# Which queue issues the weights' loads during the attention stage

## The chip, the cores and the metric

One core of one Trainium2 chip runs the whole kernel. The metric is the device time in microseconds (us) of one execution. The kernel before was timed in three runs: median 664.88 us, from 664.65 to 665.11.

## The reference

Sparse-window attention feeds two feed-forward layers, all in float32:

```python
# attention: 2 batches, 8 heads, 768 tokens, 64 columns per head
k_sum = k.reshape(B, H, 24, 32, D).max(axis=3)      # one key per block of 32
v_sum = v.reshape(B, H, 24, 32, D).mean(axis=3)     # one value per block
scores = concat(where(|i - j| < 16, q @ k.T / 8, -1e9), q @ k_sum.T / 8 + log(32))
x = softmax(scores) @ concat(v, v_sum)               # 1536 tokens x 512
# first layer, 512 -> 2048 -> 512
h = x @ w_in;  x = (h * sigmoid(1.702 * h)) @ w_out
# second layer, 512 -> 1536 -> 512
x = (sigmoid(x @ w_gate) * (x @ w_val)) @ w_out2
```

The weights arrive in a 64-bit format and every product of the layers is formed from a high and a low part of both factors.

## The kernel before, in words

**Attention** works in 24 units: two batches, three groups of 256 query rows, four pairs of heads (`units`). A unit needs its query tile (`load_q`, 256 KB, five buffers), its pair's keys (`load_k`, 400 KB for one batch and pair), a window of values (`load_v`, 768 KB for a group of units) and the block means of the values, copied into the same window (`put_v`, 256 KB, from the tile `vs`, which is computed from the loads `vt`). The steps of a unit are listed in `ORDER` with a lag each: `w_copy` (L370, GpSimd) scales the keys, `b_pe` (L379, L381, TensorE) makes the scores `ps_s`, `b_max` (L386, VectorE) the row maximum `nm`, `b_exp` (L394, ScalarE) the exponentials, `n_inv` (L401, L403, VectorE) and `n_mul` (L408, GpSimd) divide by the sum, `c_pe` (L414, TensorE) transposes, `c_copy` (L419, VectorE) copies to `pt`, `d_pe` (L429, TensorE) multiplies with the values, and `d_hi`, `d_lo` (L447, L450) split the result into `xH` and `xL`. `c_pe` and `d_pe` come three units after `b_pe`.

**Weights.** A matrix here is one piece of 256 columns or rows of a layer's weight. `fetch` (L145 to L156) issues two loads for it, `raw` (1024 KB) and `mid` (the same memory shifted by one 16-bit word, 1023 KB). `decode` (L92 to L120) makes the high and low parts from both in six VectorE steps (L104, L108, L110, L112, L117, L119) and two of ScalarE. There is one buffer `raw` and one buffer `mid`; the second matrix alone lies in `xH` and `xL`, which are still free then. `load_group` (L158) decodes the matrices in turn, and behind the second step of each decode it calls `fetch` for the matrix two places on. So the load of a matrix into `raw` must wait until VectorE has read the last one there (L104), and the load into `mid` until L108 has read it.

**The attention stage** (the first `manual_schedule` block) calls `fetch` twice ahead of its loop, for the first and the second matrix. In its loop over t from -1, `pull(2)` advances the decode, and four more fetches come out of it: the third matrix at t = 1, the fourth at t = 5, the fifth at t = 8, the sixth at t = 12. From t = 10 on `filler` puts four steps of the first layer between the units (`EARLY = 4`). The rest of both layers follows in the second block.

**Order.** SyncE's queue (SP) runs in the order of the program text: all loads of the attention but the first four query tiles, which ScalarE issues, and all fetches go through it one after another; one that waits for a buffer holds what is behind it. The other engines' instructions, GpSimd's (POOL) among them, are put in an order by a planner that simulates the program. Each engine then runs its list in that order.

Of the kernel before, what the change touches and what calls it, by code (L numbers as in the profile page):

```python
# [29 lines left out]
def attention_moe_moe2_kernel(ctx: ExitStack, tc: tile.TileContext, ins: dict, out: bass.AP):  # L30
    nc = tc.nc
# [47 lines left out]
    def pool(slots, n, name):  # L79
        p = ctx.enter_context(tc.tile_pool(name=name, bufs=n, reuse_waits="tile"))  # L80
        for s in slots:
            s.add(p, n)
        return p
# [8 lines left out]
    def decode(raw, mid, hi_out, lo_out):  # L92

        n = raw.shape[1] // 2
        head = raw.rearrange("p (n t) -> p n t", t=2)[:, :, 1]
        tail = mid.rearrange("p (n t) -> p n t", t=2)[:, :, 0]
        a, b, c = (wtmp.tile([P, n], U32, tag=f"d{x}", name=f"d{x}") for x in "abc")  # L100
        af, cf = a.bitcast(F32), c.bitcast(F32)
        ts = nc.vector.tensor_scalar

        ts(out=af, in0=head.bitcast(F32), scalar1=F64_MAX, scalar2=-F64_MAX, op0=ALU.min, op1=ALU.max)  # L104
        nc.scalar.activation(af, af, AF.Copy, scale=REBIAS)
        yield

        ts(out=b, in0=tail, scalar1=0x01FFFFFF, scalar2=None, op0=ALU.bitwise_and)  # L108
        yield
        ts(out=c, in0=a, scalar1=3, scalar2=0x7FFFF000, op0=ALU.logical_shift_left, op1=ALU.bitwise_and)  # L110
        yield
        nc.vector.scalar_tensor_tensor(  # L112
            out=c, in0=a, scalar=0x80000000, in1=c, op0=ALU.bitwise_and, op1=ALU.bitwise_or
        )
        nc.scalar.copy(hi_out, cf)
        yield
        ts(out=a, in0=c, scalar1=0xFF800000, scalar2=None, op0=ALU.bitwise_and)  # L117
        yield
        nc.vector.scalar_tensor_tensor(out=lo_out, in0=b, scalar=2.0 ** -36, in1=af, op0=ALU.mult, op1=ALU.mult)  # L119
        yield  # L120
# [8 lines left out]
    def rows_of(w, g):  # L129
        n = GF * P  # L130
        return w[g * n:(g + 1) * n, :].rearrange("(f p) e -> p f e", p=P)

    def cols_of(w, g, words):
        n = GF * P * words
        return w[:, g * n:(g + 1) * n].rearrange("(c p) e -> p c e", p=P)
# [3 lines left out]
    for layer, g in groups:  # L139
        for i, w in enumerate(mats[layer]):  # L140
            last = i == len(mats[layer]) - 1
            src = [rows_of(x, g) if last else cols_of(x, g, n) for x, n in ((w.bitcast(U32), 2), (w.bitcast(U16), 4))]
            pieces.append((f"{layer}_{g}_{i}", *src))

    def fetch():  # L145

        if pieces:
            name, src, shifted = pieces.pop(0)
            n, m = src.shape[1], src.shape[2]

            homes = ((xp, "xH"), (xp, "xL")) if name == "1_0_1" else ((wraw, "raw"), (wraw, "mid"))
            raw, mid = (p.tile([P, n * m], U32, tag=t, name=f"{t}{name}") for p, t in homes)
            nc.sync.dma_start(out=raw.rearrange("p (a n) -> p a n", a=n), in_=src)
            to = mid.bitcast(U16).rearrange("p (a n) -> p a n", a=n)
            nc.sync.dma_start(out=to[:, :, 0:2 * m - 1], in_=shifted[:, :, 1:])
            raws.append((raw, mid, (P, n, m // 2)))  # L156

    def load_group(layer, g):  # L158
        tiles = weights[layer, g] = []
        ready[layer, g] = 0  # L160
        for i in range(len(mats[layer])):
            raw, mid, shape = raws.pop(0)
            hi, lo = (w_slots.tile(list(shape), F32R, f"w{layer}_{g}_{i}{x}") for x in "HL")
            tiles += [hi, lo]
            parts = decode(raw, mid, hi.rearrange("p a n -> p (a n)"), lo.rearrange("p a n -> p (a n)"))
            for step, _ in enumerate(parts):
                if step == 1:

                    fetch()
                yield  # L170
            ready[layer, g] += 1
            yield
# [17 lines left out]
    def first(layer, g, blk, batch=False):  # L190
        w = weights[layer, g]
        gh = gh_slots.tile([P, GF, TB], F32R, f"gh{layer}_{g}_{blk}")
        gl = gl_slots.tile([P, GF, TB], F32R, f"gl{layer}_{g}_{blk}")
        gt[layer, g, blk] = gh, gl

        def sigmoid(layer, ps):
            sg = sg_slots.tile([P, TB], F32, "sg")
            nc.scalar.activation(sg, ps, AF.Sigmoid, scale=1.702 if layer == 1 else 1.0)  # L198
            return sg

        def gated(f, ps, sg):
            nc.vector.tensor_tensor(out=sg, in0=ps, in1=sg, op=ALU.mult)  # L202
            nc.scalar.copy(gh[:, f, :], sg)  # L203
            nc.gpsimd.tensor_tensor(out=gl[:, f, :], in0=sg, in1=gh[:, f, :], op=ALU.subtract)  # L204

        if batch:
            held = []
            for f in range(GF):
                held.append(project(w[0], w[1], f, blk, "ps_h"))
                yield  # L210
            held = [(ps, sigmoid(layer, ps)) for ps in held]
            yield
            for f, (ps, sg) in enumerate(held):
                gated(f, ps, sg)
            yield
            return
        for f in range(GF):
            ps = project(w[0], w[1], f, blk, "ps_h")
            sg = sigmoid(layer, ps)
            if layer == 2:  # L220
                ps = project(w[2], w[3], f, blk, "ps_v")
            gated(f, ps, sg)
            yield
# [50 lines left out]
    def pull(n):  # L274
        for _ in range(n):
            if next(coming, True):
                break

    def need(layer, g, n):
        while ready.get((layer, g), 0) < n:  # L280
            pull(1)

    with tc.manual_schedule(engines={mybir.EngineType.SP}), ExitStack() as es:
# [180 lines left out]
        for _ in range(4):  # L464
# [14 lines left out]
        sum_load(0, 3)  # L479
        load_q(4, nc.sync)  # L480
        fetch()
        fetch()
        make_identity(nc, ident)

        nc.vector.memset(mask, 0.0)
# [8 lines left out]
            out=win, in_=win, pattern=[[0, NSLOT], [1, P - W0]], compare_op=ALU.is_gt, fill=NEG,  # L494
# [3 lines left out]
            out=win, in_=win, pattern=[[0, NSLOT], [-1, P - W0]], compare_op=ALU.is_gt, fill=NEG,  # L498
# [62 lines left out]
    with tc.manual_schedule(engines={mybir.EngineType.SP}):  # L561
        pool([w_slots], 4, "w_b")
        pool([gh_slots, gl_slots], 1, "g_b")
        pool([sg_slots], 2, "sg_b")
        acc_b = ctx.enter_context(tc.tile_pool(name="acc_b", bufs=1, reuse_waits="tile"))
        ps_o = ctx.enter_context(tc.tile_pool(name="ps_o", bufs=6, space=PSUM, reuse_waits="tile"))
        o_tag = "o"
        pull(1000)
        coming = load_group(*groups[2])
        pull(1)  # L570
        prev = None
        for step in steps[EARLY:]:
            layer, g, blk = step
            need(layer, g, len(mats[layer]) - 1)
            for _ in first(*step):
                pull(1)
            if prev:
                need(*prev[:2], len(mats[prev[0]]))
                for _ in second(*prev, prev[1] == ends[prev[0]]):
                    pull(1 if groups.index((layer, g)) + 1 < n1 else 2)  # L580
            prev = step
            nxt = groups.index((layer, g)) + 1
            if nxt < len(groups) and groups[nxt] not in ready and blk == (NTB - 1 if layer == 1 and g < 2 else 0):
                pull(1000)
                coming = load_group(*groups[nxt])
        for _ in second(*prev, True):
            pass
# [40 lines left out]
```

## Time and profile before

| | |
|---|---|
| median of 3 runs | 664.88 us |
| the profiled execution's own time | 663.71 us |
| its span | 661.9 us |
| TensorE (PE) busy | 631.7 us, 95% |
| VectorE (DVE) busy | 415.2 us, 63% |
| ScalarE (ACT) busy | 243.1 us, 37% |
| GpSimd (POOL) busy | 187.2 us, 28% |
| moved by DMA | 93.97 MB, mean 142 GB/s |

The span runs from the first to the last instruction of the trace; the execution's own time is 1.8 us longer. An engine's busy share is a mean over stages with different limits, so the stages are looked at one by one. "PEclk" is the clock that TensorE was granted, as a share of full speed; a matmul at half the clock counts as busy for longer. In a row of the stages "DMA share" is how busy the 16 DMA engines were.

### The profile page before, as it was taken

What the parts mean: (1) busy time and instruction counts of PE and PEld (TensorE: products, weight loads), DVE (VectorE), ACT (ScalarE), POOL (GpSimd) and SP (SyncE); (2) the same over time, 40 slices, a digit from 0 to 9 for tenths busy, and PEclk for the clock granted to TensorE, in tenths of its full rate; (3) what the DMA queues carried; (4) which work ended last, traced back from release to release, by engine and by line L of the source; (5) the groups of instructions that cost most, each with busy time, mean ns of one, the idle gap of its engine ahead of it and who ended that gap; (6) DMA issues with size and microseconds to landing.
All of it is one profiled execution on the core that took longest, in us unless ns stands there. A gap on an engine that the chain in (4) does not pass through costs nothing.

```text
span 661.9 us, 8251 instructions
## 1 busy us (share of the span) xinstructions
PE 631.7 (95%) x3168; PEld 515.1 (78%) x3170; DVE 415.2 (63%) x604; ACT 243.1 (37%) x498; POOL 187.2 (28%) x164
## 2 busy tenths in 40 slices
PE   6478799999999999999999999999999999999997
PEld 3255688778888888888888888888888888888886
DVE  6899656559998777777778626437627627422223
ACT  3355574746443333333345425313213213211110
POOL 6574576413332222213131112111111111211110
PEclk9778899999999999999999999999999999999999
DMA  9999773007775242434333034423414413000013
GB/s 314 351 372 325 223 236 94 3 13 276 255 261 198 93 171 99 159 111 145 118 138 111 20 124 143 147 92 140 176 66 151 182 49 128 0 1 0 13 67 112
DMA packets 39672, 93.97 MB, mean 142 GB/s; under 512 B 2128, under 2 KB 12624, under 8 KB 39632
## 3 DMA queue, kind: packets, MB, share of 16 engines
q1 hardware_dynamic: 39056, 92.39, 40.3%
q10 hardware_dynamic: 576, 1.05, 0.4%
q8 instruction: 25, 0.41, 0.2%
q14 instruction: 15, 0.12, 0.1%
HBM read 88.71 MB, written 3.15 MB: 139 GB/s over the span
## 4 chain that ended last, share of the span: by engine, by line
PE 88%; DVE 3%; DMA 3%; ACT 3%; POOL 1%; issue 1%; SPq 0%; DVEq 0%; ACTq 0%; POOLq 0%
PE ps_o L181 35%; PE ps_h L181 34%; PE ps_v L181 15%; DMA mid<-in_moe_w_in 2%; PE ps_s L381 2%; PE ps_x L429 1%; PE ps_p L414 1%; ACT e L394 1%; DMA vt<-in_vt 1%; DVE nm L386 1%; POOL kx L370 0%; ACT L198 0%; ACT L394 0%; DVE dc L110 0%; DVE dc L112 0%
## 5 line engine op out<-in xcount | busy, mean ns | idle before, releaser
L204 POOL TENSOR_TENSOR gl<-sg,gh 128x512 fp32r<-128x512 f32 x84 | 116.1, 1383 | 419.4 <-ACT gh L203 419.3
L260 DVE TENSOR_TENSOR acc<-ps_o,acc 128x512 f32<-128x512 f32 x143 | 96.3, 684 | 37.2 <-PE ps_o L181 36.8
L203 ACT CAST gh<-sg 128x512 fp32r<-128x512 f32 x84 | 52.1, 621 | 134.9 <-DVE sg L202 134.9
L198 ACT ACTIVATE sg<-ps_h 128x512 f32<-128x512 f32 x84 | 49.8, 596 | 139.2 <-PE ps_h L181 139.1
L202 DVE TENSOR_TENSOR sg<-ps_v,sg 128x512 f32<-128x512 f32 x36 | 24.8, 690 | 110.5 <-PE ps_v L181 110.0
L181 PE MATMUL ps_o<-gl,w_1H 128*128 128x512 f32 x192 | 75.6, 394 | 0.7 <-POOL gl L204 0.7
L181 PE MATMUL ps_o<-gh,w_1L 128*128 128x512 f32 x192 | 75.6, 400 | 0.5 <-ACT gh L203 0.4
L181 PE MATMUL ps_h<-xL,w_0H 128*128 128x512 f32 x192 | 75.7, 394 | 0.0
L181 PE MATMUL ps_h<-xH,w_0L 128*128 128x512 f32 x192 | 75.3, 396 | 0.0
L181 PE MATMUL ps_h<-xH,w_0H 128*128 128x512 f32 x192 | 75.3, 392 | 0.0
L181 PE MATMUL ps_o<-gh,w_1H 128*128 128x512 f32 x192 | 75.1, 391 | 0.0
L181 PE MATMUL ps_o<-w_2L,gh 128*128 128x512 f32 (+1 forms) x146 | 56.4, 386 | 0.0
L181 PE MATMUL ps_o<-w_2H,gl 128*128 128x512 f32 (+1 forms) x146 | 56.4, 386 | 0.0
L181 PE MATMUL ps_o<-w_2H,gh 128*128 128x512 f32 (+1 forms) x146 | 56.4, 386 | 0.0
L181 PE MATMUL ps_h<-yH,w_0L 128*128 128x512 f32 x144 | 56.0, 389 | 0.0
L181 PE MATMUL ps_h<-yL,w_0H 128*128 128x512 f32 x144 | 56.0, 389 | 0.0
L181 PE MATMUL ps_h<-yH,w_0H 128*128 128x512 f32 x144 | 56.0, 389 | 0.0
L181 PE MATMUL ps_v<-yH,w_1L 128*128 128x512 f32 x144 | 56.0, 389 | 0.0
L181 PE MATMUL ps_v<-yL,w_1H 128*128 128x512 f32 x144 | 56.0, 389 | 0.0
L181 PE MATMUL ps_v<-yH,w_1H 128*128 128x512 f32 x144 | 56.0, 389 | 0.0
L202 DVE TENSOR_TENSOR sg<-ps_h,sg 128x512 f32<-128x512 f32 x48 | 32.8, 685 | 30.1 <-ACT sg L198 30.1
L112 DVE SCALAR_TENSOR_TENSOR dc<-da,dc 128x1024 uint32<-128x1024 uint32 x34 | 48.6, 1429 | 0.5
(80 smaller groups left out, 1077.0 us busy)
## 6 DMA issues: line engine op xcount, KB each, us to landing
raw<-in_moe_w_out SPq DMA_DIRECT2D x13, 1024.0 KB, 4.9
mid<-in_moe_w_out SPq DMA_DIRECT2D x13, 1023.5 KB, 6.8
raw<-in_moe_w_in SPq DMA_DIRECT2D x8, 1024.0 KB, 5.3
mid<-in_moe_w_in SPq DMA_DIRECT2D x8, 1023.0 KB, 7.2
raw<-in_moe_w_gate SPq DMA_DIRECT2D x6, 1024.0 KB, 5.1
raw<-in_moe_w_val SPq DMA_DIRECT2D x6, 1024.0 KB, 5.0
mid<-in_moe_w_gate SPq DMA_DIRECT2D x6, 1023.0 KB, 7.1
mid<-in_moe_w_val SPq DMA_DIRECT2D x6, 1023.0 KB, 7.1
```

What stands on the lines that cost most here:

```text
L112: nc.vector.scalar_tensor_tensor(out=c, in0=a, scalar=0x80000000, in1=c, op0=ALU.bitwise_and, op1=ALU.bitwise_or)
L181: nc.tensor.matmul(ps, lhsT=a, rhs=b, start=i == 0, stop=i == n - 1)
L198: nc.scalar.activation(sg, ps, AF.Sigmoid, scale=1.702 if layer == 1 else 1.0)
L202: nc.vector.tensor_tensor(out=sg, in0=ps, in1=sg, op=ALU.mult)
L203: nc.scalar.copy(gh[:, f, :], sg)
L204: nc.gpsimd.tensor_tensor(out=gl[:, f, :], in0=sg, in1=gh[:, f, :], op=ALU.subtract)
L260: nc.vector.tensor_tensor(out=a[:, m, :], in0=ps, in1=a[:, m, :], op=ALU.add)
L381: nc.tensor.matmul(ps[:, j, :], lhsT=t[:, j, :], rhs=kt[:, j, :], start=False, stop=j == G - 1)
L386: nc.vector.tensor_reduce(out=nm, in_=live["s", u], axis=AX.X, op=ALU.max, negate=True)
L394: nc.scalar.activation(e[:, j, :], s[:, j, :], AF.Exp, bias=nm[:, j:j + 1], accum_out=sm[:, j:j + 1])
L414: nc.tensor.transpose(ps[:, j, :], e[:, j, :], ident)
L429: nc.tensor.matmul(ps[64 * e:64 * e + 64, j, :], lhsT=vw(b, g * G + j)[:, h * D:(h + 1) * D], rhs=t[:, j, 64 * e:64 * e + 64], start=True, ...
```

## The change

A list of one element holds the queue that `fetch` issues from. It is SyncE's for the first two fetches, GpSimd's from then until the decodes of the first two groups are all called up at the end of the attention, and SyncE's again after that. Four fetches, eight loads, change their queue: those of the third to the sixth matrix. What they load, where to and behind what they must wait does not change.

```diff
+    queue = [nc.sync]
+
     def fetch():
...
-            nc.sync.dma_start(out=raw.rearrange("p (a n) -> p a n", a=n), in_=src)
+            queue[0].dma_start(out=raw.rearrange("p (a n) -> p a n", a=n), in_=src)
             to = mid.bitcast(U16).rearrange("p (a n) -> p a n", a=n)
-            nc.sync.dma_start(out=to[:, :, 0:2 * m - 1], in_=shifted[:, :, 1:])
+            queue[0].dma_start(out=to[:, :, 0:2 * m - 1], in_=shifted[:, :, 1:])
...
         load_q(4, nc.sync)
         fetch()
         fetch()
+        queue[0] = nc.gpsimd
         make_identity(nc, ident)
...
         pull(1000)
+        queue[0] = nc.sync
         coming = load_group(*groups[2])
```

## Rows read from the trace of the kernel before

**Rows 1.** Busy time by stage: stretch, length, engines (instructions), granted clock, DMA share, GB/s.
```profile
24.30:29.80 5.50, 0.08 (x2) 0.06 (x1) 5.29 (x7) 1.40 (x2) 1.57 (x2) 0.50 1.04 363
29.80:41.00 11.20, 7.52 (x53) 6.39 (x54) 9.39 (x15) 5.29 (x20) 5.71 (x5) 0.51 1.06 308
41.00:60.00 19.00, 13.90 (x131) 10.55 (x131) 18.77 (x38) 11.23 (x41) 11.15 (x11) 0.94 1.03 339
...
70.90:74.00 3.10, 0.18 (x8) 0.13 (x3) 3.10 (x6) 3.07 (x11) 1.33 (x1) 1.00 0.94 177
74.00:80.00 6.00, 5.59 (x32) 3.59 (x32) 2.06 (x5) 1.82 (x4) 5.08 (x6) 0.72 0.40 96
80.00:140.00 60.00, 58.97 (x474) 48.20 (x477) 30.79 (x70) 38.14 (x126) 33.18 (x36) 1.00 0.37 106
140.00:662.00 522.00, 518.03 (x2316) 428.67 (x2314) 318.64 (x407) 167.09 (x241) 107.20 (x77) 1.00 0.33 119
```

**Rows 2.** TensorE's waits in 0 to 150 us: total, times, longest.
```profile
PE ps_s L381 <- DMA q<-in_q: 7.1, 4, 5.4
PE ps_s L379 <- ACT e L394: 6.1, 5, 2.9
...
PE ps_x L429 <- DMA vwin<-vs: 2.2, 1, 2.2
```

**Rows 3.** SyncE's queue in time: start us, length us of the issue, line, load.
```profile
15.67 1.21 SPq L312 DMA_DIRECT2D q<-in_q  x1
...
20.94 1.39 SPq L329 DMA_DIRECT2D vwin<-vs  x2
...
23.28 0.89 SPq L153 DMA_DIRECT2D raw<-in_moe_w_in  x1
25.84 1.21 SPq L155 DMA_DIRECT2D mid<-in_moe_w_in  x1
28.42 5.93 SPq L312 DMA_DIRECT2D q<-in_q  x4
39.67 0.38 SPq L153 DMA_DIRECT2D raw<-in_moe_w_out  x1
42.37 0.38 SPq L155 DMA_DIRECT2D mid<-in_moe_w_out  x1
42.80 0.46 SPq L312 DMA_DIRECT2D q<-in_q  x1
```

**Rows 4.** Loads issued at 15.67, 21, 25.84 us, one each: us to landing.
```profile
q<-in_q SPq DMA_DIRECT2D x1, 256.0 KB, 14.0
...
vwin<-vs SPq DMA_DIRECT2D x1, 256.0 KB, 13.0
...
mid<-in_moe_w_in SPq DMA_DIRECT2D x1, 1023.0 KB, 15.8
```

**Rows 5.** Loads of two queues issued in 2.2 to 2.75 us: us to landing.
```profile
k<-in_k SPq DMA_DIRECT2D x1, 400.0 KB, 7.6
q<-in_q ACTq DMA_DIRECT2D x1, 256.0 KB, 7.9
```

**Rows 6.** VectorE in time, decode steps that free or need weights' buffers.
```profile
24.79 0.66 DVE L108 TENSOR_SCALAR db<-mid 128x1024 uint32<-128x1024 uint32 x1
...
38.95 0.69 DVE L104 TENSOR_SCALAR da<-raw 128x1024 f32<-128x1024 f32 x1 [0.20 <-DMA raw<-in_moe_w_in]
...
41.65 0.69 DVE L108 TENSOR_SCALAR db<-mid 128x1024 uint32<-128x1024 uint32 x1
```

**Rows 7.** GpSimd in time, 23 to 42 us; in brackets idle before and its releaser.
```profile
23.53 1.04 POOL L408 TENSOR_TENSOR e<-e,rr 128x512 f32<-128x512 f32 x1
25.04 1.30 POOL L408 TENSOR_TENSOR e<-e,rr 128x512 f32<-128x512 f32 x1 [0.48 <-DVE rr L403]
31.98 1.41 POOL L370 TENSOR_SCALAR kx<-k 128x384 f32<-128x384 f32 x1 [5.63 <-PE ps_s L381]
33.35 1.32 POOL L370 TENSOR_SCALAR kx<-ks 128x128 f32<-128x128 f32 x1
...
40.64 0.53 POOL L370 TENSOR_SCALAR kx<-ks 128x128 f32<-128x128 f32 x1
```

## The prediction, made before the change was run

> **What bounds the kernel now.** I read the busy times by stage first. From 80 us to the end TensorE is the bound: 58.97 of 60 us and then 518.03 of 522 us, at full clock, while the DMA engines are at 0.37 and 0.33 [rows 1]. What happens there is a fixed amount of TensorE work, so the kernel's time changes by as much as TensorE is ahead or behind at about 80 us. Ahead of that three things are short at once. The DMA engines are full from 24.3 to 60 us (share 1.03 to 1.06; over 1 because the share is rough), VectorE is busy for 5.29 of 5.5, 9.39 of 11.2 and 18.77 of 19 us, and TensorE stands: 5.42 us idle in the first of these stretches, 3.68 in the second, 5.10 in the third, and its clock is at 0.50 and 0.51, the lower of its two levels, in the first two [rows 1]. The list of TensorE's waits names the loads: 7.1 us for query tiles, 2.2 us for the block means in the window [rows 2]. The reader is to see in SyncE's queue that these loads are issued long before they are needed (q at 15.67, vs at 20.94) [rows 3] and take 14.0 and 13.0 us to land [rows 4]: they stand behind other bytes, not behind a late issue. So the order of bytes decides in this stretch, not the instant of issue.
>
> **The change, part by part.** *What moves.* Eight issues leave SyncE's queue for GpSimd's. The third matrix now is issued at 23.28 and 25.84 us [rows 3], behind q and vs in one line, and its second half lands at 25.84 + 15.8 = 41.6 us [rows 4]; VectorE takes it at once, at 41.65 [rows 6].
>
> *Overtaking.* On a queue of its own the third matrix no longer stands behind q and vs. The one place where two queues have loads under way together is the start: a load of SyncE and one of ScalarE, issued within half a microsecond, land after 7.6 and 7.9 us [rows 5], so neither queue goes first. I take it that two queues share the engines about evenly. The buffer `raw` was free before 23.28, and GpSimd is between two operations at 24.6 and free at 26.3 [rows 7]; `mid` is free when L108 ends at 25.45 [rows 6]. So I let the third matrix start at 26. Its 2.10 MB take 2.10 / 0.363 = 5.8 us of all engines at the rate of 24.3 to 29.8, 6.8 at the 308 GB/s of the next stretch [rows 1]; middle 6.3. The query tile that lands at 15.67 + 14.0 = 29.7 has 3.7 us to go at 26 and becomes 3.7 later, 33.4. The block means, which land at 21 + 13.0 = 34.0, have 8 us to go; by then the whole third matrix has gone in between, so they land 6.3 later, at 40.3. Nothing behind the matrix in the old line gets later by it. TensorE's d_pe of the first unit, which waits for vs, shifts by 6.3 us, and with it the copies and results on VectorE.
>
> *How much of this costs.* VectorE is what the stretch 24 to 60 us is made of, so the price is the time by which VectorE stands. It is nothing if the planner fills the hole with the third matrix's decode, which is then there 4 us sooner and is some 5.8 us of work (24.3 to 29.8 holds five of a decode's six steps in 5.29 us, and L104 adds 0.69) [rows 1, 6]. It is 6.3 us if VectorE's list stays as it is. It can be a small gain, 0.2 us for the wait of L104 [rows 6] and no more than 1.81, all of VectorE's idle time in 29.8 to 41 [rows 1]. A list made for one simulated order rarely fits a hole wholly; I take the middle, +3.
>
> *GpSimd's time.* Eight issues. The trace has no issue of this queue; below stands SyncE's shortest, 0.38 us [rows 3], above I set GpSimd's dearest row, 1.41 us [rows 7], so 3 to 11.3 us of GpSimd. It is idle for 3.9 of 5.5, 5.5 of 11.2 and 7.9 of 19 us [rows 1], which hides most of it. If that cover is gone, w_copy or n_mul is late next and TensorE behind it. Bounds 0 and 11.3; nearest to the idle time, +0.5.
>
> *SyncE's queue freed.* It now stands from the end of four query issues, 28.42 + 5.93 = 34.35, to 39.67, until L104 has read `raw`, and again to 42.37 for `mid`; only then comes the next query tile at 42.80 [rows 3]. These stalls go, and the loads behind the fourth and fifth matrix no longer stand behind 2.1 MB; sharing instead, they land up to half of 6.3, 3 us, sooner. What that can give back is TensorE's idle stretch at 70.9 to 74, 2.92 us, with the 0.41 idle and the slow clock behind it, 5.59 x (1 - 0.72) = 1.6 [rows 1]: 4.9 at most. But that stretch ends with a wait for an exponential, not for a load [rows 2], so I take -1. Below, 0.
>
> *Sum.* +3 + 0.5 - 1 = +2.5 us on the profiled execution: 663.71 + 2.5 = 666.2. The median of the runs is 1.17 above that execution, so the forecast on its scale is 664.88 + 2.5 = 667.4. All lower ends together are -1.8 - 4.9 = -6.7, all upper ends +17.6.
>
> The Trainium skill's page "SBUF — State Buffer", section on the two separate sides, warns against this very change: loads issued by GpSimd need descriptors that its cores write, and VectorE's instructions in a two-port mode lock these cores out meanwhile. The trace shows something of this kind: the same 128x128 operation of GpSimd took 1.32 us at 33.35, in VectorE's decode, and 0.53 at 40.64 [rows 7]. With 0.8 us more on each of eight issues GpSimd's term would have 6.3 us more to hide. No run here shows the descriptors themselves.
>
> **The rivals.** *No change.* The bytes are the same and the engines are full; VectorE's list takes the third matrix's decode into the hole whole, and the attention is later by what the decode is sooner. For it: VectorE has no free time in 41 to 60 us (0.23) [rows 1], so work moved ahead of 41 is not lost. Against it: the first unit's d_pe holds all later units through two `pt` buffers. Time 664.9. The skill's "DMA: Bandwidth & Descriptors", section on issuing engines not being separate queues, says the same: loads from all issuers interleave on the same 16 engines, only issue time is saved.
>
> *Faster: the weights yield.* One mechanism in one place: GpSimd's list. Its next operation after 26.3 is w_copy at 31.98, which waits 5.63 us for TensorE's scores [rows 7]. If the third matrix's loads stand behind it in the planner's list, they start at 34.7, when vs has landed; nothing is overtaken, and the four query tiles issued from 28.42 on [rows 3], which stood behind this matrix, land some 6 us sooner instead. Start after 34.0: gain; before 29.7: loss; that is the point from which it decides. Price: VectorE's 1.81 us of idle time in 29.8 to 41, and some of the 4.9 above, together -3: 661.9. For it: the wait is long. Against: the loads are ready eight microseconds sooner, and a planner that puts ready work first takes them first.
>
> *Slower by more: GpSimd is held.* A load that waits for VectorE's read at the head of GpSimd's list holds n_mul and w_copy as it held SyncE, 5.3 us at 39.67 [rows 3]. One such wait on top of half the overtaking, less what the freed queue gives: +6, 670.9. Against it: n_mul waits for VectorE too, mostly for later instructions.
>
> **How the numbers follow.** The forecast of 667.4 has 0.40 (its own range 664.5 to 670), no change 0.20, the yielding weights 0.27, the held GpSimd 0.13. Most of the forecast's unknown is what the planner does with VectorE's list, and that reaches both neighbours. About 0.2%, 1.3 us, is what a measurement can tell from no change. Faster: 0.27 and a little of the no-change case, 0.28. Same: 0.16 of the no-change case and 0.06 of the forecast's low end, 0.22. Slower: the rest, 0.50. The range from 661.0 to 671.0 takes in the rivals' times and leaves out the sum's upper end, for which GpSimd would have to have no idle time.
>
> **What would show it.** Right: a load of the third matrix issued by GpSimd before 27 us; the query tile that took 14.0 us to land takes about 18; TensorE's wait for vs ends near 40; the third matrix's L108 is ready before 41.6 on VectorE; after 80 us the stages are as long as before. Wrong: vs lands at 34 or sooner, or VectorE has no hole between 34 and 42, or GpSimd's own operations wait behind its issues, or the stage behind 140 us changes its length.

## The result: slower by 1.5%, nearly four times the forecast's step

The changed kernel takes 674.38 us, the one before 664.77 beside it: 9.6 us more, at a ratio of 1.0148 (95%: 1.0135 to 1.0162), where +2.5 were forecast and the range ended at 671.0. The sign was right and the size wrong. The span grew from 661.9 to 672.4 us. One execution of the third matrix alone (1280.69 us) and one of both late moves (715.45 us), further down, ran in a much slower state and are left out of the ratios.

The stages of the kernel after, with the columns of [rows 1]:

```profile
24.30:29.80 5.50, 0.00 (x0) 0.00 (x0) 5.33 (x6) 1.10 (x2) 3.30 (x4) 0.73 1.03 394
29.80:41.00 11.20, 2.99 (x24) 2.72 (x24) 7.22 (x9) 3.86 (x11) 1.97 (x2) 0.50 1.04 291
41.00:60.00 19.00, 14.62 (x124) 12.05 (x120) 15.23 (x32) 7.63 (x31) 13.76 (x13) 0.83 0.68 213
60.00:70.90 10.90, 8.72 (x69) 6.30 (x70) 10.20 (x18) 7.23 (x29) 5.76 (x5) 0.69 1.01 349
70.90:74.00 3.10, 2.54 (x15) 1.43 (x14) 1.62 (x3) 0.00 (x0) 1.66 (x2) 1.00 1.03 400
74.00:80.00 6.00, 3.37 (x28) 2.63 (x27) 3.23 (x6) 0.96 (x2) 2.61 (x3) 0.83 0.64 241
80.00:140.00 60.00, 57.55 (x463) 45.76 (x464) 37.10 (x78) 40.35 (x134) 38.81 (x41) 0.99 0.44 126
```

The kernel before in the one stage that [rows 1] leaves out:

```profile
60.00:70.90 10.90, 10.90 (x95) 7.83 (x93) 9.61 (x18) 5.24 (x14) 4.33 (x5) 0.95 1.05 381
```

Against [rows 1] the reader is to see three things. From 29.8 to 41 us TensorE works 2.99 us instead of 7.52, and VectorE 7.22 instead of 9.39: both stand. From 41 to 60 the DMA engines, full before (1.03), have a hole (0.68), and VectorE has 3.77 us idle instead of 0.23. And TensorE, which lacked 1.03 us in 80 to 140 before, now lacks 2.45.

Where the time is lost can be estimated from these rows: busy time times granted clock is TensorE's work in us at full clock. The kernel after falls behind by 2.4 us from 24.3 to 41, 0.9 to 60, 3.2 to 80 and 2.0 to 140: 8.5 us in all, of the 10.5 by which the two profiled executions differ. So more than half is lost behind 60 us, where the clock is lower too (0.69 instead of 0.95 from 60 to 70.9).

TensorE's waits in 0 to 150 us (total, times, longest), beside [rows 2], and the two waits in time:

```profile
PE ps_s L384 <- DMA q<-in_q: 8.3, 3, 7.2
PE ps_x L432 <- DMA vwin<-vs: 6.6, 1, 6.6
```
```profile
31.42 2.05 PE L384 MATMUL ps_s<-kx,q 128*128 128x128 f32 x8 [7.22 <-DMA q<-in_q]
40.06 1.12 PE L432 MATMUL ps_x<-pt,vwin 128*64 128x64 f32 x16 [6.59 <-DMA vwin<-vs]
```

The same product with the block means started at 34.01 before. It is 6.05 us later; the next six such products start 5.35 to 7.6 us later than theirs before (39.24 becomes 46.85, 62.62 becomes 69.63), and the eighth to the tenth 11.6 to 13.2 (79.27 becomes 90.83). Between the seventh and the eighth the trace names a second late load, the last value sums `vt` of the second batch:

```profile
76.36 0.95 DVE L345 TENSOR_REDUCE vm<-vt 128x24 f32<-128x768 f32 x1 [3.28 <-DMA vt<-in_vt]
```
```profile
77.37 0.41 PE L355 MATMUL ps_v<-ident,vm 128*32 128x128 f32 x2 [2.62 <-DVE vm L345]
77.79 0.98 PE L432 MATMUL ps_x<-pt,vwin 128*64 128x64 f32 x16
```

SyncE issued this load at 58.81 us, and it took 17.5 us to land; before it was issued at 59.00 and took 10.3. The fifth matrix's loads, which GpSimd issued at 60.94 and 66.98, landed at 72.2 and 76.1, ahead of it.

GpSimd's issues of the third matrix, and its and the window's times to landing (the number at the end of a row is us from issue):

```profile
23.43 0.96 POOL L156 DMA_DIRECT2D raw<-in_moe_w_in  x1
27.21 0.91 POOL L158 DMA_DIRECT2D mid<-in_moe_w_in  x1
```
```profile
q<-in_q SPq DMA_DIRECT2D x1, 256.0 KB, 15.6
...
vwin<-vs SPq DMA_DIRECT2D x1, 256.0 KB, 19.0
...
raw<-in_moe_w_in POOLq DMA_DIRECT2D x1, 1024.0 KB, 9.8
...
mid<-in_moe_w_in POOLq DMA_DIRECT2D x1, 1023.0 KB, 11.9
```

So the third matrix lands at 33.2 and 39.1 us, and the block means, issued at 21.0, at 40.0; before it was 34.0 for the means and 41.6 for the matrix's second half [rows 3, 4]. SyncE's queue in time, and its waits:

```profile
21.01 1.39 SPq L332 DMA_DIRECT2D vwin<-vs  x2
22.49 21.80 SPq L315 DMA_DIRECT2D q<-in_q  x6
44.39 0.38 SPq L338 DMA_DIRECT2D vt<-in_vt  x1
```
```profile
SPq L315 <- PE ps_s L384: 32.6, 8, 18.9
```

The six query issues stretch over 21.8 us: SyncE, free of the weights, stands for 18.9 us in one wait for a query buffer that TensorE has not read yet. The DMA engines' hole begins there (share 0.69 from 41 to 44.4 us). Its deepest part, 0.22 from 53 to 57, lies in a second wait of SyncE, 8.4 us to 55.29, for the window, which late products still read; and the fourth matrix, issued at 39.67 and 42.37 before, is issued by GpSimd at 48.21 and 55.49 only. VectorE in time:

```profile
36.45 1.22 DVE L119 SCALAR_TENSOR_TENSOR w_1L<-db,da 128x1024 fp32r<-128x1024 uint32 x1
41.23 0.69 DVE L422 COPY pt<-ps_p 128x512 f32<-128x512 f32 x1 [3.55 <-PE ps_x L432]
...
43.98 0.69 DVE L389 TENSOR_REDUCE nm<-ps_s 128x4 f32<-128x512 f32 x1 [1.57 <-PE ps_s L384]
46.11 0.69 DVE L389 TENSOR_REDUCE nm<-ps_s 128x4 f32<-128x512 f32 x1 [1.44 <-PE ps_s L384]
...
46.76 0.66 DVE L104 TENSOR_SCALAR da<-raw 128x1024 f32<-128x1024 f32 x1
...
50.68 0.77 DVE L108 TENSOR_SCALAR db<-mid 128x1024 uint32<-128x1024 uint32 x1
```

VectorE waits 3.55, 1.57 and 1.44 us while the third matrix lies in its buffers, the first half since 33.2. Its decode starts at 46.76, behind the late attention, though it stood at 38.95 before [rows 6]. VectorE's operations up to the reduction at 43.98 come in the same order as before; then a second reduction stands ahead of the decode, where the decode stood first. The list did not fill the hole.

### The profile page after: what moved, and what is told of

Same layout as the page of the kernel before. It is cut to its first block, busy times and chain, and to the rows that moved or that the text cites. A ratio compares the mean times of both kernels' runs of the same rounds, so it can differ in the third digit from the quotient of the medians.

```text
span 672.4 us, 8259 instructions
## 1 busy us (share of the span) xinstructions
PE 633.3 (94%) x3169; PEld 516.1 (77%) x3170; DVE 418.5 (62%) x604; ACT 242.7 (36%) x498; POOL 194.3 (29%) x172
## 4 chain that ended last, share of the span: by engine, by line
PE 85%; DMA 9%; DVE 3%; ACT 2%; issue 0%; SPq 0%; POOL 0%; DVEq 0%; ACTq 0%
PE ps_o L184 33%; PE ps_h L184 33%; PE ps_v L184 15%; DMA q<-in_q 4%; DMA k<-in_k 2%; PE ps_s L384 2%; DMA vwin<-vs 1%; PE ps_x L432 1%; DMA vt<-in_vt 1%; PE ps_p L417 1%; ACT e L397 1%; ACT L201 1%; DVE nm L389 0%; DVE sg L205 0%; DVE dc L112 0%
```

## Experiments

All edits are to the kernel before. In the diffs, N is the number of matrices fetched so far, `eng` the queue that both loads of `fetch` are issued from, and `(layer, g, i)` the matrix whose decode is being called up. Differences in us are worked out from the ratios: so much of the kernel before (the whole change: 0.0148 x 664.77 = 9.8).

**Which of the four matrices, and GpSimd or the second queue?**

```diff
     def fetch():
+        eng = nc.gpsimd if N == 2 else nc.sync          # e1_third_only, e12_third_only_again
+        eng = nc.gpsimd if 3 <= N < 6 else nc.sync      # e2_fourth_to_sixth
+        eng = nc.scalar if 2 <= N < 6 else nc.sync      # e3_scalar_queue
```

Third only: 

> Only the third matrix's two loads go to GpSimd's queue; the fourth to sixth stay with SyncE. Theory (overtaking: the third matrix takes half of the DMA engines from the query tile and the block means that were ahead of it): TensorE's wait for the block means grows from 2.2 to about 6 us, they land near 40 us instead of 34, and the time is 5 to 7 us above the kernel before (670 to 672). Rival (GpSimd's issues themselves cost, about 1.2 us each over eight): two of eight issues, 2 to 3 us above (667). If the loss came from the later matrices, no change.

Measured 670.98 against 665.35, 1.0082 (1.0065 to 1.0098): +5.5 us.

Fourth to sixth only: 

> The third matrix stays with SyncE, the fourth to sixth go to GpSimd's queue. Theory (overtaking): the block means land at 34 us as before, nothing is lost before 40 us; what is left is the late fourth matrix (issued 8 us later by GpSimd's list in the changed kernel) and the fifth matrix overtaking keys and value sums of the second batch: 2 to 4 us above the kernel before (667 to 669). Rival (the issues themselves): six of eight, about 7 us above (672).

Measured 669.56, 1.0063 (1.0041 to 1.0084). The wait for the block means is 2.4 us, as before, and the time is lost nevertheless: more than half of the loss is the third matrix's, the rest is not.

All four from ScalarE's queue: 

> The same four matrices are issued by ScalarE's queue, a second queue in hardware, and GpSimd has nothing to do with it. Theory (overtaking by any second queue): the block means land about 6 us later than before, 40 instead of 34, and the time is 6 to 10 us above the kernel before (671 to 675). Rival (GpSimd's issues and descriptors): as the kernel before within 1.5 us, and the means land at 34.

Measured 673.98, 1.0145 (1.0116 to 1.0174): as slow as GpSimd's queue. A loss of this size comes without GpSimd. But the issues now stand in ScalarE's list instead, so the run does not show that GpSimd's time costs nothing. The way differs, too: ScalarE issued `mid` only at 34.26, the first product with the means waited less and started at 36.18, and the delay grew to 7.2 us by the seventh.

```profile
36.18 1.12 PE L429 MATMUL ps_x<-pt,vwin 128*64 128x64 f32 x16 [4.67 <-DMA vwin<-vs]
```

**The other way round: attention's loads overtake.**

```diff
-        def put_v(b, g):
+        def put_v(b, g, eng=nc.sync):                  # its load is issued by eng
...
-                load_q(t + 5, nc.sync)
+                load_q(t + 5, nc.gpsimd if t < 2 else nc.sync)
...
-                put_v(0, 0)
+                put_v(0, 0, nc.gpsimd)
```

> The other way round: all weights stay with SyncE, and the query tiles of t = 0 and 1 and the first window's block means are issued by GpSimd's queue, so that they overtake the first two matrices. Theory: the block means land before 28 us, the query tile before 27, TensorE does not stand at 24 to 34, and the time falls by 3 to 6 us (659 to 662). Rival (GpSimd's issues cost, three here): 2 to 4 us slower than the kernel before (667 to 669).

Measured 673.89, 1.0129 (1.0112 to 1.0146): against the theory. TensorE no longer waits for the means at all, but for ScalarE's exponentials and VectorE's copies; its waits in 0 to 150 us:

```profile
PE ps_s L379 <- ACT e L394: 10.7, 8, 3.5
PE ps_p L414 <- DVE pt L419: 10.1, 4, 4.9
```

The planner had made new lists, in which decode steps stand ahead of the attention's copies: VectorE's third copy `pt` (41.33 us) comes behind two steps of the third matrix (38.68 and 40.72), while before it came ahead of them (36.67 and 38.95), and TensorE's longest wait for a copy, 4.9 us, ends there. So the bytes' order is not the whole account: an edit to a queue also changes the engines' lists, and that can outweigh what the bytes gain. How much of the loss is the lists' and how much GpSimd's three issues cost was not separated.

**One at a time among the later three.**

```diff
     def fetch():
+        eng = nc.gpsimd if N == 3 else nc.sync          # e5_fourth_only
+        eng = nc.gpsimd if 4 <= N < 6 else nc.sync      # e6_fifth_and_sixth
```

> Only the fourth matrix's two loads go to GpSimd's queue. Theory (order of bytes): it overtakes three or four query tiles near 40 us, whose buffers the units need one by one, and its own issue waits in GpSimd's list: 1 to 2 us above the kernel before (666 to 667). Rival (any change makes the planner write other lists for VectorE and TensorE, and other lists cost 4 to 5 us): 669 to 670.

Measured 665.73 against 664.39, 1.0014 (1.0002 to 1.0026): +0.9 us.

> Only the fifth and sixth matrix go to GpSimd's queue; neither is needed before the attention ends. Theory (order of bytes): the fifth overtakes the keys and value sums of the second batch near 55 to 65 us, 2 to 3 us above the kernel before (667 to 668), and with the fourth alone the two sum to what the fourth to sixth together cost, 4.2 us. Rival (other lists): 669 to 670 here too.

Measured 668.21, 1.0044 (1.0031 to 1.0057). The third, the fourth and the last two alone add up to 5.5 + 0.9 + 2.9 = 9.3 us against the whole's 9.8.

**The third matrix's bytes moved within SyncE's one queue.**

```diff
                 if step == 1 and (layer, g, i) != (1, 0, 0):
                     fetch()
...
+                fetch()                                 # e7_one_queue_overtaken
                 put_v(0, 0)
...
+            if t == 4:                                  # e8_third_later, behind load_q
+                fetch()
```

Ahead of the block means: 

> All loads stay with SyncE; the third matrix's two loads are put ahead of the first window's block means in SyncE's order, so it overtakes them without any second queue. Theory (order of bytes): the means land at 39 to 40 us instead of 34, TensorE waits 5 to 6 us for them, and the time is 5 to 7 us above the kernel before (670 to 672). Rival (a second queue costs in itself, by sharing or by its issue): the kernel before within 1.5 us.

Measured 670.07 against 664.39, 1.0074 (1.0058 to 1.0090).

```profile
41.60 1.12 PE L429 MATMUL ps_x<-pt,vwin 128*64 128x64 f32 x16 [4.34 <-DMA vwin<-vs]
```

No second queue and nothing of GpSimd: with the third matrix's bytes ahead of the means the product is at 41.60 and the kernel loses 4.9 us, nearly what the third matrix loses on GpSimd's queue. So the order of the bytes, with the lists that the planner makes for it, is enough for this half of the loss.

Behind the query tiles: 

> All loads stay with SyncE; the third matrix's loads move behind the four query tiles that stood behind them (from t = 1 to t = 4), so the weights yield instead of overtake. Theory (order of bytes alone decides): the query tiles land near 37 us instead of 41 to 43, and the time falls by 1 to 3 us (662 to 664). Rival (VectorE's work between 40 and 60 us is as short as the loads, and the third matrix's decode comes later): no gain, 665 to 669.

Measured 665.67, 1.0016 (1.0007 to 1.0026): later bytes of the third matrix give back nothing, the product is at 33.52.

**Once more the third alone, for its profile** (one run; the edit is the first of all).

> The third matrix alone on GpSimd's queue once more, for its trace. Theory (overtaking): the block means land near 40 us, TensorE waits 5 to 6 us for them, and from 42 us on the DMA engines are no longer full, since the third matrix is through and SyncE's next loads wait for buffers that the late units hold: a DMA share below 0.8 in 41 to 60 us, where it was 1.03. Rival (the later matrices make that hole): 1.0 there.

Measured 671.62. The product with the means, and the stage 41 to 60:

```profile
40.31 1.12 PE L429 MATMUL ps_x<-pt,vwin 128*64 128x64 f32 x16 [8.33 <-DMA vwin<-vs]
```
```profile
41.00:60.00 19.00, 15.16 (x136) 13.02 (x134) 15.23 (x33) 9.47 (x39) 14.27 (x12) 0.78 0.71 254
```

The late means, VectorE's 3.77 us of idle time and most of the DMA engines' hole come with the third matrix alone. Behind 60 us the two kernels part:

```profile
60.00:70.90 10.90, 7.45 (x69) 4.62 (x66) 9.26 (x18) 5.23 (x21) 3.68 (x5) 0.96 1.05 325
70.90:74.00 3.10, 3.10 (x14) 2.30 (x14) 2.41 (x5) 1.26 (x2) 1.19 (x2) 0.59 1.05 396
74.00:80.00 6.00, 5.49 (x41) 3.69 (x40) 5.72 (x10) 2.49 (x11) 3.00 (x2) 1.00 0.95 298
```

By the same estimate as for the result, with the same stages of its trace, the third matrix alone loses 2.2 us from 24.3 to 41, 1.2 to 60, 0.1 to 80 and 2.0 to 140. What the other three matrices add, 3.1 us, lies between 60 and 80 us, where the value sums land late.

**The fifth and the sixth apart, and the fifth in one queue.**

```diff
     def fetch():
+        eng = nc.gpsimd if N == 4 else nc.sync          # e13_fifth_only
+        eng = nc.gpsimd if N == 5 else nc.sync          # e14_sixth_only
...
-                if step == 1:
+                if step == 1 and (layer, g, i) != (1, 1, 0):     # e15_fifth_one_queue
                     fetch()
...
+            if t == 8:
+                fetch()
             if 0 <= t < NU - 5:
```

> Only the fifth matrix's two loads go to GpSimd's queue. Theory (order of bytes): it overtakes the second batch's keys and value sums; it carries the whole price of the fifth and sixth together, 2 to 4 us above the kernel before (667 to 669). Rival (other lists of the planner): any price, without a reason for the fifth to carry it all.

Measured 667.52 against 664.53, 1.0045 (1.0027 to 1.0063): the fifth alone, +3.0 us, loses as much as the last two together, +2.9.

> Only the sixth matrix's two loads go to GpSimd's queue. When it can be issued, from 66 us on, the DMA engines have room and what it could overtake is not waited for. Theory (order of bytes): the kernel before within 1.3 us. Rival (other lists): 2 us or more away from it, to either side.

Measured 665.71, 1.0015 (1.0004 to 1.0026).

> All loads with SyncE; the fifth matrix's loads are put ahead of the query tile, value sums and keys of t = 8, so it overtakes them in one queue. Theory (order of bytes): 2 to 4 us above the kernel before (667 to 669), as when GpSimd issues it. Rival (GpSimd's queue or the lists it brings): no change.

Measured 665.39, 1.0015 (0.9997 to 1.0032): not shown to cost anything, though SyncE issues the fifth's first load at 51.55, sooner than GpSimd did (52.94). So the order of the bytes by itself does not account for the 3.0 us. The trace with the fifth on GpSimd's queue shows another price. Its GpSimd and VectorE, then VectorE in the one-queue run:

```profile
52.94 0.95 POOL L153 DMA_DIRECT2D raw<-in_moe_w_in  x1 [2.41 <-DVE nm L386]
53.92 1.05 POOL L408 TENSOR_TENSOR e<-e,rr 128x512 f32<-128x512 f32 x1
55.84 0.79 POOL L155 DMA_DIRECT2D mid<-in_moe_w_in  x1 [0.87 <-DVE rr L403]
```
```profile
53.10 2.43 DVE L108 TENSOR_SCALAR db<-mid 128x1024 uint32<-128x1024 uint32 x1
56.98 0.76 DVE L401 TENSOR_SCALAR rs<-sm 128x4 f32<-128x4 f32 x1
```
```profile
52.51 0.84 DVE L108 TENSOR_SCALAR db<-mid 128x1024 uint32<-128x1024 uint32 x1
54.79 0.15 DVE L401 TENSOR_SCALAR rs<-sm 128x4 f32<-128x4 f32 x1
```

Beside GpSimd's issues and the operation behind each, two of VectorE's instructions take 2.43 and 0.76 us instead of 0.84 and 0.15 (as in the kernel before). From 50 us to the copy `pt` at 59.39 (56.49 before) VectorE's order is that of the kernel before, so these two account for 2.2 of the 2.9 us by which the copy is late, and the sixth product starts 3.3 us late. The run with the fifth and the sixth shows the same (1.92 and 0.76 us). Later the lists differ as well: the first reduction of a key tile after 58 us is at 75.48 instead of 62.35, and at 71.39 in the one-queue run, which loses little.

**If order decides, move weights behind the attention's loads.**

```diff
-                if step == 1:
+                if step == 1 and (layer, g, i) not in ((1, 1, 0), (1, 1, 1)):   # e9, e11, e16
                     fetch()
...
+            if t in (12, 16):
+                fetch()
...
         load_q(4, nc.sync)                              # e10, e11, e16
         fetch()
-        fetch()
...
                 put_v(0, 1)
+                fetch()
```

Fifth and sixth later: 

> All loads with SyncE; the fifth and sixth matrix, which nothing needs before the attention ends, move from t = 8 and 12 to t = 12 and 16, behind the keys and value sums of the second batch. Theory (order of bytes): the reverse of what the fifth matrix did when it overtook: keys and sums land up to 6 us sooner, 1 to 3 us faster than the kernel before (662 to 664). Rival (VectorE is as short there, and every other list is worse): the same or 1 to 3 us slower.

Measured 671.90 against 665.46, 1.0102 (1.0080 to 1.0125): against the theory. The stretch 60 to 74 us is gained, TensorE is busy throughout, but from 74 to 80 it works 2.05 us instead of 5.59 [rows 1] while ScalarE is full:

```profile
74.00:80.00 6.00, 2.05 (x12) 1.22 (x11) 3.33 (x7) 5.94 (x18) 3.29 (x4) 0.98 1.01 362
```
```profile
70.52 1.28 ACT L198 ACT_TABLE_LOAD   x1
72.43 1.28 ACT L394 ACT_TABLE_LOAD   x1
75.25 1.28 ACT L198 ACT_TABLE_LOAD   x1
77.94 1.28 ACT L394 ACT_TABLE_LOAD   x1
```

ScalarE's new list goes back and forth between two functions, at 1.28 us for a table each time (seven loads up to 165 us, five before), and TensorE waits for it:

```profile
77.97 0.73 PE L181 MATMUL ps_o<-gh,w_1L 128*128 128x512 f32 x2 [1.88 <-ACT gh L203]
80.79 0.59 PE L379 MATMUL ps_s<-mask,pick 128*128 128x512 bf16 x1 [2.08 <-ACT e L394]
```

From 80 to 90 us TensorE's granted clock is 0.67, where it was 1.00 before. How much of the 6.8 us these waits make up was not measured.

Second matrix behind the first block means: 

> All loads with SyncE; the second matrix's two loads move behind the first window's block means (from ahead of the loop to t = 0), so the query tile that landed at 29.7 us and the means that landed at 34 have 2.1 MB less ahead of them. Theory (order of bytes): they land near 23 and 28 us, TensorE does not stand at 24 to 34, 2 to 5 us faster (660 to 663). Rival (VectorE is as short there; the second matrix's decode, then later, holds the units instead): within 1.5 us of the kernel before or slower by up to 5.

Measured 662.04, 0.9959 (0.9942 to 0.9975).

```profile
28.90 1.12 PE L429 MATMUL ps_x<-pt,vwin 128*64 128x64 f32 x16 [1.50 <-DMA vwin<-vs]
```

The product with the means is 5.1 us sooner and the kernel faster by 2.7: a better order of the bytes goes with a gain, too.

Both: 

> Both moves together: the second matrix behind the first block means, the fifth and sixth behind the second batch's keys and sums; all loads with SyncE. Theory (order of bytes): the gains add up, 3 to 7 us faster than the kernel before (658 to 662). Rival (VectorE as short): within 1.5 us or slower.

Measured 657.88, 0.9884 (0.9856 to 0.9912).

> The second matrix behind the first block means, the fifth and sixth behind the second batch's keys and sums, all with SyncE, once more for its trace: 656 to 660 us, the means land near 28 us, TensorE is busy for more than 10 of the 16.7 us from 24.3 to 41 us (7.6 in the kernel before), by the order of bytes. If instead the planner's lists are what helps, the means land no sooner and TensorE gains only behind 60 us.

Measured 657.82 against 664.53, 0.9893 (0.9876 to 0.9911): 7.1 us faster than the kernel before, and the fastest of all with its twin. Its first product with the means and the stages 24.3 to 80:

```profile
29.52 1.12 PE L429 MATMUL ps_x<-pt,vwin 128*64 128x64 f32 x16 [3.36 <-DMA vwin<-vs]
```
```profile
24.30:41.00 16.70, 9.99 (x85) 7.85 (x86) 14.59 (x23) 5.94 (x15) 5.87 (x6) 0.59 1.04 328
41.00:60.00 19.00, 16.71 (x135) 13.46 (x132) 16.68 (x34) 11.13 (x46) 12.22 (x12) 0.82 0.97 316
60.00:80.00 20.00, 17.68 (x146) 12.71 (x144) 15.25 (x29) 13.20 (x34) 11.02 (x12) 1.00 0.98 307
```

Before, TensorE worked 7.60, 13.90 and 16.68 us in these three. The later fifth and sixth alone cost 6.8 us; together with the later second they cost nothing, and more is gained than by the second alone. The two edits do not add up, which fits lists that are made anew for each.

## Why the prediction was wrong, point by point

**Overtaking: right for the block means.** vs was to land at 40.3 us and d_pe to shift by 6.3; it landed at 40.0 and shifted 6.05, with the loads issued at 23.4 and 27.2 instead of both at 26. The query tile, to land at 33.4, landed at 31.3: it lost 1.6 us, not 3.7. So the even sharing of two queues, taken from [rows 5], is not borne out: it is off for the query tile, and the means' time asks only that the whole third matrix goes in ahead of them. "Nothing behind the matrix in the old line gets later by it" did not hold for the later matrices: the last value sums took 17.5 us to land instead of 10.3. Nor did "after 80 us the stages are as long as before": an estimated 2.0 us are lost from 80 to 140.

**"SyncE's queue freed": the step that failed most.** It stood in the sum as -1. The fourth to the sixth matrix, whose move was to bring this gain, alone measure +4.2: 5.2 of the 7.3 us between the forecast's +2.5 and the measured 9.8. The stalls for `raw` and `mid` went, and a wait of 18.9 us for a query buffer came: those buffers come free only when TensorE has read them, and TensorE was late. With attention late, the freed queue had no load that it could issue. The fifth matrix was priced only as a gain "up to half of 6.3, 3 us, sooner" for the loads around it. Alone it measures +3.0, the fourth +0.9 and the sixth +1.0.

**"How much of this costs": the other step that failed, by size.** It chose +3, the middle between a hole that VectorE fills and one that it does not. VectorE kept its order up to the hole, the third's L104 came 7.8 us later instead of sooner, and the upper end, 6.3, was the nearer one. The third matrix alone measures +5.5 by its ratio, and its bytes alone, in one queue, +4.9. The reason that stood in the same sentence ("a list made for one simulated order rarely fits a hole wholly") spoke for the end, not for the middle.

**GpSimd's time: sized on the wrong engine.** The eight issues took 6.5 us together, between the bounds of 3 and 11.3, and GpSimd's idle time was to hide them. The price seen is VectorE's: beside the issues of the fifth matrix alone its instructions took 2.2 us longer, where the whole term was +0.5. For the third matrix little is left for it (+5.5 on GpSimd's queue, +4.9 in one queue).

**The rivals.** "GpSimd is held" had the nearest time, 670.9. What it describes is in the trace of the fifth alone: the issue at 52.94 has waited 2.41 us at the head of GpSimd's list, with n_mul behind it, which was at 51.65 in the kernel before and is at 53.92. But it was reckoned with a wait of the fourth matrix, and that does not show: GpSimd issues its first load at 48.21 with no idle time ahead of it, and the fourth alone costs 0.9 us. So the near time is luck. "The weights yield" fell: GpSimd issued the first load at 23.43, long before w_copy. "No change" fell with its condition, that VectorE's list takes the decode into the hole. Its rule from the Trainium skill, "DMA: Bandwidth & Descriptors", section "Issuing engines are not separate DMA queues", is borne out in that loads from two queues interleave. GpSimd's loads of the third matrix landed at 33.2 and 39.1 us, between SyncE's query tile at 31.3 and means at 40.0, both issued ahead of them. That an added queue changes only the time of issuing was not so here: it gave up the order in which the loads had been issued, and the means landed 6 us later.

**What the mechanism does not settle.** The first product's delay does not fix the loss one for one: 7.6 us of it cost 4.9 in one queue, and 2.2 us cost 9.6 with ScalarE's queue. How the whole change's loss beyond the third matrix's divides among late value sums, VectorE's longer instructions and new lists is open.

## What to carry to other kernels

Where the DMA engines were full, a load landed behind the bytes issued ahead of it in its queue, and a second queue gave that order up. Work out what the moved bytes overtake, for every moved load and not for the first alone, and try to put loads in the order of need instead. Take a hole as filled only if another engine's list has ready work at that place; here the price was close to its whole length. An issue on another engine's list is not free because that engine is idle: look at what runs beside it. Where a planner makes the lists, any change of a load makes new ones, so two edits are timed together before either is dropped: one here cost 6.8 us alone and none beside the other.

## What the hardware showed that was not expected

A 1 MB load cost GpSimd 0.76 to 0.96 us to issue in the changed kernel, where SyncE's shortest took 0.38 (the kernel before) and ScalarE's 0.37 (all four from its queue). VectorE's instructions beside such an issue and GpSimd's next operation can take longer: 2.43 us instead of 0.84, and in the changed kernel 1.37 us at 61.48 for a tile of 128x4 that took 0.15 at 58.97. A delay of GpSimd's loads by VectorE did not show: the third matrix, issued by GpSimd beside SyncE's loads, landed 9.8 and 11.9 us after its issues with the DMA engines at 1.03 and 1.04 of their time, though VectorE was busy for 7.30 us of the 8 from 26 to 34. TensorE's granted clock was 0.73 in 24.3 to 29.8, where TensorE did nothing after the change, and 0.50, the lower of its levels, in 29.8 to 41, where it worked 2.99 us; before it was 0.50 and 0.51 there, with 7.52 us of work in the second stretch [rows 1].
